# Reordering the beginning of a fused spectral-filter and MLP kernel: one load queue, shared evacuations, transpose mode, and the places of the weight conversions

## The chip, the cores and the metric

One core of one Trainium2 chip. The metric is the device time of one execution in microseconds (us); lower is better. The profile is one execution recorded by the hardware profiler; its times are microseconds from the span's start.

## The reference

Eight batches of 3008 rows by 256 columns go through a circular convolution along the rows (a real FFT, a product with a complex filter, the inverse FFT), and every row of the result then through a two-layer MLP with the hard-swish function between:

```python
X = np.fft.rfft(x, axis=1)                       # x: (8, 3008, 256)
Y = X * (filt_r + 1j * filt_i)[None, :, :]       # filters: (1505, 256)
y = np.fft.irfft(Y, n=x.shape[1], axis=1)
h = y.reshape(24064, 256) @ w_in                 # w_in: (256, 2048)
g = h * np.clip(h + 3.0, 0.0, 6.0) / 6.0
out = g @ w_out                                  # w_out: (2048, 256)
```

All data are FP32.

## The kernel before

The FFT of length 3008 = 47 × 64 is done as matrix products with small trigonometric tables: a first transform over the 47 (`wa`), a second over the 64 (`wb`), the product with the filter, and two transforms back (`wi`, then `wai`). Between these the data pass through scratch memory in DRAM (`z_d` between the first two, `g_d` between the last two)[...]. The MLP works on blocks of 512 tokens and, within a block, on eight slices of 256 hidden channels: one slice of one block is a step, and there are 47 × 8 steps. Block 0 is computed plainly (`plain_up`, L537, and `plain_down`, L548); from block 1 on a Strassen form with seven products in place of eight is used (L450 and L526). It needs sums of weight parts, which GpSimd forms (`w_sums`, L252). The work of the following batches' transforms is put into the steps by a plan written out by hand: `at(step, fn, ...)` lists what each step also does, functions in `EARLY` before the second half of the step's matmuls and the others behind them. [...]

The change touches only what comes before block 0 and the plan of block 0 with the first steps of block 1. The beginning has these stages.

- Loads: the start table with an identity matrix and the first-transform table, `x` of batch 0 (`x0_load`, L291, in pieces of 4 or 8 of the 32 column pairs), filter and `wb` tables for six groups (`table_load`, L178 to L181), raw weights (`w_load`, L215), `wi`, `wai` and `wa`. Sync, ScalarE and GpSimd all issue loads. Groups 2 to 5 of the tables go into memory where `x` of batch 0 lay, so they wait until it has been read.
- First transform of batch 0 (`a0_unit`, L300): eight units of 8 matmuls; each unit fills two PSUM banks out of four, and ScalarE copies them out (L302).
- For each of six groups: `turn` (L312: eight 128×128 matmuls with the identity as the moving operand, which transpose the data; ScalarE copies out, L314), `b_unit` (L355), `f_unit` (product with the filter on VectorE, L367 to L369), `bi_unit` (L387; copied out at L390) and `g_store` (L396, to DRAM).
- `t4_load` (L418) brings the stored data back in another layout, `n_unit` (L425; copied out at L431) does the last transform for the first chunks of tokens. `keep_warm` (L643) issues matmuls on zeros while TensorE has nothing else.
- Weights: 16 parts have to be converted before they are used (`w_conv`, L226 to L245: the bits of a pair of words are put together to one FP32 number; seven or eight VectorE operations of 128×512 for each part, and with `act` one on ScalarE). Part 2p is `w_in` of slice p, part 2p + 1 `w_out`. A part's raw bits wait in buffers of other tiles (`W_AT`), and a buffer takes the next part only when the one before it has been converted: that wait stands on the queue that issues the load.

Before the change three parts are converted beside the first transform, two beside the last transform, and eleven in block 0, two in each step from the first on (`at(i // 2, convert, 1)`). In block 0, a step's hswish (L500, VectorE, two for each step) reads the PSUM bank that the next step's `plain_up` writes, so the next step cannot begin before the hswish has run, and the hswish stands on VectorE behind the conversions of the step before last.

Of the kernel before, what the change touches and what calls it, by code (L numbers as in the profile page):

```python
# [23 lines left out]
NA = 47  # L24
NC = 64
KH = 24
# [81 lines left out]
def kernel(  # L108
# [60 lines left out]
    def table_load(b, c, qs=(nc.sync, nc.sync)):  # L169
        if b == 0 and c >= FB:  # L170

            at = x0_at(1536 * (c - FB), 1536)
            t, wb = at[:, 0:1024].rearrange("p (k d) -> p k d", k=TC), at[:, 1024:].rearrange("p (k m) -> p k m", k=TC)
        else:
            t, wb = ft[(b * NT + c) % FB], tabp.tile([P, TC, P], FP32, name="wb")
        st["ft", b, c] = t
        for q, src, p0 in ((qs[0], filt_r, 0), (qs[1], filt_i, HALF)):
            q.dma_start(t[p0:p0 + 32, :, :].rearrange("p k d -> p (k d)"),  # L178
                              raw(src, c * TC, [[NA * D, 32], [1, TC * D]]))
            q.dma_start(t[p0 + 32:p0 + 64, :, :], raw(src, NA - c * TC, [[NA * D, 32], [-D, TC], [1, D]]))  # L180
        qs[c % 2].dma_start(wb, wb_d[:, ts(c, TC), :])  # L181
        st["wb", b, c] = wb
# [103 lines left out]
    def x0_load(j, n):  # L286
        rows = x[0].rearrange("(a c) d -> a c d", c=NC)
        nc.vector.memset(x0[32:64, j:j + n, :], 0.0)
        for a, m in (0, 32), (32, NA - 32):
            for h, q in ((0, nc.sync), (1, nc.gpsimd)):  # L290
                q.dma_start(x0[h * 64 + a:h * 64 + a + m, j:j + n, :], rows[a:a + m, ds(h * HC + j, n), :])  # L291

    def zt(dh):
        return (xn.rearrange("p a n -> p (a n)"), xs.rearrange("p i j d -> p (i j d)"))[dh]

    def a0_unit(j):
        for dh in range(2):
            ps = bank(0)
            for u in range(4):
                nc.tensor.matmul(ps[:, ts(u, P)], x0[0:64 + NA, j + u, ts(dh, P)], st["start"][0:64 + NA, ts(1, P)],  # L300
                                 start=True, stop=True)
            nc.scalar.activation(out=zt(dh).rearrange("p (n j) -> p j n", j=HC)[:, j:j + 4, :],  # L302
                                 in_=ps.rearrange("p (j n) -> p j n", j=4)[:, :, 0:4 * KH], func=AXT.Copy)

    def turn(c):
        t = t2p.tile([P, TC, D], FP32, name="t2")
        for v in range(2):
            ps = psU.tile([P, 512], FP32, name=("al", "be")[v])
            for u in range(2):
                for dh in range(2):  # L310
                    k = c * TC + 2 * v + u
                    nc.tensor.matmul(ps[:, ds(u * D + dh * P, P)], zt(dh)[:, ts(k, P)], st["start"][:, 0:P],  # L312
                                     start=True, stop=True)
            nc.scalar.activation(out=t[:, 2 * v:2 * v + 2, :].rearrange("p k d -> p (k d)"), in_=ps, func=AXT.Copy)  # L314
# [65 lines left out]
    def bi_unit(b, i):  # L380
        ys = [st.pop(("y", b, i + v)) for v in range(2)]
        ps = [psF.tile([P, 2, D], FP32, name="psf", tag="f") for ri in range(2)]
        for v in range(2):
            for ri in range(2):

                w, y = (wi[ts(ri, 64), 0, :], ys[v][ts(ri, 64)]) if b else (wi[:, 1 + ri, :], ys[v][ri])
                nc.tensor.matmul(ps[ri][ts(v, 64)], w, y, start=True, stop=True)  # L387
# [5 lines left out]
    def g_store(b, i, qs=(nc.gpsimd, nc.gpsimd)):  # L393
        t = st.pop(("t3", b, i))
        for v in range(2):
            qs[v].dma_start(g_d[b, i + v].rearrange("ri u c d -> c (ri u) d"), t[ts(v, 64)].rearrange("p ri u d -> p (ri u) d"))  # L396
# [219 lines left out]
    with tc.manual_schedule():  # L616
# [4 lines left out]
        two = (nc.sync, nc.gpsimd)  # L621
# [5 lines left out]
        nc.vector.memset(half_c, 0.5)  # L627
        loaded = done = 0

        def convert(n, act=True, most=NCONV, q=nc.sync):  # L630
            nonlocal loaded, done
            for i in range(n + 1):
                while loaded < most and w_before(loaded) < done:
                    w_load(loaded, q)
                    loaded += 1
                if i < n:
                    w_conv(done, act)
                    done += 1
# [6 lines left out]
        convert(0, most=2, q=nc.scalar)  # L645
        nc.scalar.dma_start(wi, wi_d)
        nc.scalar.activation(out=zero[:, 0:1], in_=half_c, func=AXT.Copy)
        keep_warm(5)
        for j, n in (0, 4), (4, 4), (8, 8), (16, 8), (24, 8):
            x0_load(j, n)  # L650
        convert(0, most=3, q=nc.gpsimd)
        nc.gpsimd.memset(t4, 0.0)
        for c in range(FB):
            table_load(0, c, two)
        for j in range(0, HC, 4):
            a0_unit(j)
        convert(3, False, 5)
        for c in range(FB, NT):
            table_load(0, c, two)
        convert(0, most=8)  # L660
        nc.sync.dma_start(wai[:, 0:8, :], wai_d[:, 0:8, :])
        for i in range(3):
            w_sums(i, False)
        turn(0)
        for c in range(NT + 1):
# [6 lines left out]
            if c:  # L672
                bi_unit(0, 2 * c - 2)
                g_store(0, 2 * c - 2, (nc.scalar, nc.scalar) if c < NT else (nc.scalar, nc.sync))
# [3 lines left out]
        keep_warm(16)  # L678
        convert(2, False)
# [3 lines left out]
        for c in range(3):  # L683
            x_load(1, c)
        nc.sync.dma_start(wai[:, 8:HC, :], wai_d[:, 8:HC, :])
        nc.sync.dma_start(wa, wa_d)
        for i in 3, 4:
            w_sums(i, False)


        for i in range(NCONV - done):
            at(i // 2, convert, 1)
            at(i // 2 + 1, w_sums, done + i, False)
        for p in range(NP):
            for i in range(2):
                at(p + 2, w_sums, 2 * p + i, True)

# [17 lines left out]
        def places(n):  # L715
# [6 lines left out]
            if n == 1:  # L722
                a_at = list(range(1, NB + 1))
# [126 lines left out]
```

## Time and profile before

| | |
|---|---|
| median of 3 runs | 2766.2 us (2765.32 to 2770.9) |
| span of the profiled execution | 2764.2 us |
| TensorE matmuls busy | 2716.7 us (98%) |
| VectorE busy | 1951.5 us (71%) |
| ScalarE busy | 1332.9 us (48%) |
| GpSimd busy | 408.4 us (15%) |
| DMA | 194.74 MB, mean 70 GB/s |
| first matmul of `plain_up` / first matmul of block 1 | 89.06 / 166.16 us |

Busy shares are means over the whole span. The change concerns the first 170 us or so, so the views that count are those of that stretch: the chain of waits in order of time (start, length, engine and line of each piece), the timeline (start, length, engine, line, operation, and in brackets the idle time before it and what ended it), and the windows (for each stretch the busy time of each engine with its instructions, the granted TensorE clock, the share of the DMA engines and the GB/s). Each FP32 matmul shows as two rows of TensorE.

### The profile page before, as it was taken

The numbers are of one execution on the slowest core, as the hardware profiler recorded it, in microseconds if no ns is written. First come the engines' busy times: TensorE is split into PE (matmuls) and PEld (weight loads), VectorE is DVE, ScalarE is ACT, GpSimd is POOL, SyncE is SP. The second block draws the span as 40 slices with busy tenths as digits, with TensorE's granted clock in tenths as the row PEclk, the third lists the DMA queues.
The fourth block names the chain that finished last, engine by engine and source line by source line (L and its number), as shares of the span: only waits on it lengthen the run. The fifth ranks groups of instructions, "written<-read, shape, count | busy, mean of one in ns | idle before, by whom it ended". The sixth has DMA issues, their size and how long they took to land.

```text
span 2764.2 us, 47162 instructions
## 1 busy us (share of the span) xinstructions
PE 2716.7 (98%) x18154; PEld 2412.4 (87%) x18154; DVE 1951.5 (71%) x3404; ACT 1332.9 (48%) x2665; POOL 408.4 (15%) x640
## 2 busy tenths in 40 slices
PE   8999999999999999999999999999999999999997
PEld 6478888999889988899889998899988999999997
DVE  7657766777567775678756787567775777766665
ACT  4234455444554455544554445544455444545443
POOL 2341112010211002110121001210012100100000
PEclk9999999999999999999999999999999999999999
DMA  8633223221332213322133212332123321100000
GB/s 220 169 100 89 60 70 88 62 76 50 85 91 70 60 41 89 89 73 54 46 92 90 69 50 56 91 100 69 35 60 91 92 72 38 42 24 24 18 9 16
DMA packets 117827, 194.74 MB, mean 70 GB/s; under 512 B 21805, under 2 KB 82349, under 8 KB 117193
## 3 DMA queue, kind: packets, MB, share of 16 engines
q1 hardware_dynamic: 94397, 138.68, 17.7%
q0 software_dynamic: 19088, 48.65, 7.7%
q10 hardware_dynamic: 4118, 4.39, 0.6%
q8 instruction: 144, 2.36, 0.4%
q14 instruction: 80, 0.66, 0.1%
HBM read 119.80 MB, written 71.83 MB: 69 GB/s over the span
## 4 chain that ended last, share of the span: by engine, by line
PE 93%; DVE 3%; DMA 2%; issue 0%; ACT 0%; SPq 0%; POOL 0%; ACTq 0%; POOLq 0%; DVEq 0%
PE po L526 42%; PE al L450 23%; PE be L450 17%; PE psn L425 4%; PE psf L355 3%; PE psf L332 2%; PE psf L387 2%; DMA w_all<-wb_t 1%; DVE g L500 0%; DMA w_all<-in_x_dram 0%; PE po L548 0%; PE po L300 0%; PE al L537 0%; DMA t<-g_tmp 0%; DVE y L229 0%
## 5 line engine op out<-in xcount | busy, mean ns | idle before, releaser
L526 PEld LDWEIGHTS po<-w_all,g 128*128 128x128 f32 x10304 | 1369.5, 192 | 142.6 <-issue 38.3
L526 PE MATMUL po<-w_all,g 128*128 128x128 f32 x10304 | 1399.6, 276 | 4.4 <-DVE g L500 4.4
L500 DVE SCALAR_TENSOR_TENSOR g<-r,h 128x512 f32<-128x512 f32 x736 | 506.7, 688 | 269.5 <-ACT r L495 257.0
L495 ACT ACTIVATE r<-h,half_c 128x512 f32<-128x512 f32 x736 | 531.2, 722 | 329.7 <-DVE h L476 317.7
L450 PE MATMUL al<-xt,w_all 128*128 128x256 f32 x2208 | 660.5, 381 | 2.1 <-DVE h L481 1.6
L476 DVE TENSOR_TENSOR h<-be,s 128x512 f32<-128x512 f32 x368 | 254.2, 691 | 264.8 <-PE be L450 253.5
L450 PE MATMUL be<-xn,w_all 128*128 128x256 f32 x1472 | 437.8, 379 | 0.0
L450 PEld LDWEIGHTS al<-xt,w_all 128*128 128x128 f32 x2208 | 335.5, 192 | 4.1 <-DVE h L481 2.3
L450 PEld LDWEIGHTS be<-xn,w_all 128*128 128x128 f32 x1472 | 279.7, 190 | 37.9
L490 ACT ACTIVATE h<-al 128x256 f32<-128x256 f32 x368 | 141.3, 384 | 350.3 <-PE al L450 350.3
L481 DVE TENSOR_TENSOR h<-al,s 128x256 f32<-128x256 f32 x368 | 156.3, 425 | 166.1 <-PE al L450 164.9
L508 DVE TENSOR_TENSOR g<-g 128x512 f32<-128x512 f32 x368 | 255.1, 693 | 12.7
L471 ACT ACTIVATE s<-al 128x256 f32<-128x256 f32 x368 | 141.4, 384 | 200.3 <-PE al L450 200.3
L462 ACT ACTIVATE s<-be 128x256 f32<-128x256 f32 x368 | 141.4, 384 | 176.3 <-PE be L450 176.3
L450 PE MATMUL al<-xn,w_all 128*128 128x256 f32 x736 | 219.9, 381 | 0.5 <-ACT h L490 0.5
L450 PE MATMUL be<-xt,w_all 128*128 128x256 f32 x736 | 218.9, 379 | 0.0
L344 POOL DMA_DIRECT2D z_tmp<-t x224 | 130.2, 585 | 421.4 <-ACT t L335 393.6
L461 ACT ACTIVATE s<-al 128x256 f32<-128x256 f32 x368 | 141.4, 384 | 70.9 <-PE al L450 70.9
L510 DVE TENSOR_TENSOR g<-g 128x256 f32<-128x256 f32 x368 | 160.6, 436 | 12.5
L507 DVE TENSOR_TENSOR g<-g 128x256 f32<-128x256 f32 x368 | 156.8, 426 | 12.6
L450 PEld LDWEIGHTS be<-xt,w_all 128*128 128x128 f32 x736 | 139.8, 190 | 18.9
L582 POOL TENSOR_TENSOR o<-p,o 128x256 f32<-128x256 f32 x45 | 32.7, 728 | 813.1 <-ACT t L390 381.1
(121 smaller groups left out, 1908.8 us busy)
## 6 DMA issues: line engine op xcount, KB each, us to landing
t<-g_tmp SPq DMA_DIRECT2D x188, 120.0 KB
z_tmp<-t POOLq DMA_DIRECT2D x224, 96.0 KB, 3.1
t<-z_tmp SPq DMA_DIRECT2D x42, 512.0 KB
g_tmp<-t POOLq DMA_DIRECT2D x84, 256.0 KB, 3.8
out_dram<-o SPq DMA_DIRECT2D x321, 47.0 KB
xs<-in_x_dram SPq DMA_DIRECT2D x112, 128.0 KB
ft<-in_filt_r_dram SPq DMA_DIRECT2D x88, 128.0 KB
wb<-wb_t SPq DMA_DIRECT2D x43, 256.0 KB
```

The costliest lines, as they stand in the source:

```text
L450: nc.tensor.matmul(ps, w_in[p][:, w, :], x, start=start, stop=stop, skip_group_check=True)
L461: nc.scalar.activation(out=s[:, 0, :], in_=al, func=AXT.Copy)
L462: nc.scalar.activation(out=s5, in_=be[:, 1, :], func=AXT.Copy)
L471: nc.scalar.activation(out=s[:, 1, :], in_=al, func=AXT.Copy)
L476: nc.vector.tensor_tensor(out=st["h"][0].rearrange("p (a n) -> p a n", a=2), in0=be, in1=s, op=ALU.add)
L481: nc.vector.tensor_tensor(out=st["h"][1][:, 256:512], in0=al, in1=s5, op=ALU.add)
L495: nc.scalar.activation(out=r, in_=st["h"][i], func=AXT.Relu, bias=half_c, scale=1.0 / 6.0)
L500: nc.vector.scalar_tensor_tensor(out=st["g", k, p][:, o:o + 2, :].rearrange("p a n -> p (a n)"), in0=st["r", i], scalar=1.0, in1=st["h"][i ...
L507: v.tensor_tensor(out=g[:, G1, :], in0=g[:, G3, :], in1=g[:, G22, :], op=ALU.add)
L508: v.tensor_tensor(out=g[:, G3:G2 + 1:2, :], in0=g[:, G3:G1 + 1, :], in1=g[:, G11:G11 + 1, :].broadcast_to([P, 2, 256]), op=ALU.subtract)
L510: v.tensor_tensor(out=g[:, G4, :], in0=g[:, G12, :], in1=g[:, G2, :], op=ALU.subtract)
L526: nc.tensor.matmul(st["po", k][bank][:, part, u, :], g[:, a, ts(u, P)], w_out[p][:, w, :], start=(p == 0 and n in OPENS and u == 0), stop= ...
```

## The change

It has five parts. Line numbers of the changed kernel are some 3 to 17 higher.

- All loads up to block 0 go out from Sync, in the order in which they are used; before, they were split between Sync, GpSimd and ScalarE. `x` is loaded in eight equal pieces, with weight part 0 behind the second and part 1 behind the fourth. Two zero fills for padding rows move from VectorE to GpSimd.
- VectorE copies out some of the PSUM banks: those with `dh` = 1 of the first transform, except in units 8 and 12, and one bank of the first `turn`.
- `turn` uses TensorE's transpose mode (`nc.tensor.transpose`) in place of a matmul with the identity.
- Two conversions are beside the first transform and three beside the last, and eleven in block 0 again, at other steps: 0, 0, 1, 2, 2, 3, 4, 4, 5, 5, 6.
- Smaller moves: the matmuls of `bi_unit` fill one bank first and then the other; both halves of each `g_store` of batch 0 go out from ScalarE; the loads of `x` of batch 1 and of the rest of `wai` are put into the plan; the first transform of batch 1 begins at step 2 in place of 1; `keep_warm` has 2 and 9 matmuls in place of 5 and 16.

The diff, cut to its core:

```diff
-        nc.vector.memset(x0[32:64, j:j + n, :], 0.0)
         for a, m in (0, 32), (32, NA - 32):
-            for h, q in ((0, nc.sync), (1, nc.gpsimd)):
-                q.dma_start(x0[...], rows[...])
+            for h in range(2):
+                nc.sync.dma_start(x0[...], rows[...])
...
-            nc.scalar.activation(out=zt(dh)..., in_=ps..., func=AXT.Copy)
+            copy(dh and j not in (8, 12), zt(dh)..., ps...)
...
-                    nc.tensor.matmul(ps[...], zt(dh)[:, ts(k, P)], st["start"][:, 0:P],
-                                     start=True, stop=True)
-            nc.scalar.activation(out=t[...], in_=ps, func=AXT.Copy)
+                    nc.tensor.transpose(ps[...], zt(dh)[:, ts(k, P)], st["start"][:, 0:P])
+            copy(c == 0 and v == 1, t[...], ps)
...
-        for v in range(2):
-            for ri in range(2):
+        for v, ri in ((0, 0), (1, 0), (0, 1), (1, 1)):
...
-        convert(0, most=2, q=nc.scalar)
-        nc.scalar.dma_start(wi, wi_d)
         nc.scalar.activation(out=zero[:, 0:1], in_=half_c, func=AXT.Copy)
-        keep_warm(5)
-        for j, n in (0, 4), (4, 4), (8, 8), (16, 8), (24, 8):
-            x0_load(j, n)
-        convert(0, most=3, q=nc.gpsimd)
-        nc.gpsimd.memset(t4, 0.0)
+        nc.scalar.dma_start(wi, wi_d)
+        keep_warm(2)
+        for j in range(0, HC, 4):
+            x0_load(j, 4)
+            load_bits({4: 1, 12: 2}.get(j, 0))
         for c in range(FB):
-            table_load(0, c, two)
+            table_load(0, c)
+        load_bits(3)
         for j in range(0, HC, 4):
             a0_unit(j)
-        convert(3, False, 5)
+            convert(j in (4, 12), False)
+        nc.gpsimd.memset(t4, 0.0)
         for c in range(FB, NT):
-            table_load(0, c, two)
-        convert(0, most=8)
+            table_load(0, c)
+            if c == 3:
+                load_bits(4)
+        load_bits(5)
         nc.sync.dma_start(wai[:, 0:8, :], wai_d[:, 0:8, :])
+        load_bits(8)
+        nc.sync.dma_start(wa, wa_d)
...
-                g_store(0, 2 * c - 2, (nc.scalar, nc.scalar) if c < NT else (nc.scalar, nc.sync))
+                g_store(0, 2 * c - 2, nc.scalar)
...
-        keep_warm(16)
-        convert(2, False)
+        keep_warm(9)
+        convert(3, False)
...
-        for c in range(3):
-            x_load(1, c)
-        nc.sync.dma_start(wai[:, 8:HC, :], wai_d[:, 8:HC, :])
-        nc.sync.dma_start(wa, wa_d)
-        for i in 3, 4:
+        for i in range(2, done):
             w_sums(i, False)
-        for i in range(NCONV - done):
-            at(i // 2, convert, 1)
-            at(i // 2 + 1, w_sums, done + i, False)
+        at(0, x_load, 1, 0)
+        for i, s in enumerate((0, 0, 1, 2, 2, 3, 4, 4, 5, 5, 6)):
+            at(s, convert, 1)
+            at(s + 1, w_sums, done + i, False)
...
+        at(0, wai_load)
+        for c in 1, 2:
+            at(c, x_load, 1, c)
...
-                a_at = list(range(1, NB + 1))
+                a_at = list(range(2, NB + 2))
```

## The prediction

> **What bounds the kernel now.** I read the page first, for the chain of waits of the whole span, and then only the beginning, since the edits end with token block 0: the chain in order of time, the timeline, and windows of 10 us.
>
> The page says that TensorE carries the span:
>
> ```profile
> PE 93%; DVE 3%; DMA 2%; issue 0%; ACT 0%; SPq 0%; POOL 0%; ACTq 0%; POOLq 0%; DVEq 0%
> ```
>
> The first matmul of block 1 starts at 166.16 us. The remaining 2,598 us are TensorE back to back in both kernels, so what the beginning loses or gains goes one to one into the end. The chain shows where those 166 us go (start, length, what):
>
> ```profile
> 5.84 10.99 DMA w_all<-in_x_dram
> 16.97 10.67 PE po L300 x79
> 27.64 16.29 DMA w_all<-wb_t
> 44.07 1.97 PE po L355 x8
> 46.04 0.89 PE al L312 x8
> 46.93 0.89 PE be L312 x8
> 47.82 1.87 PE psf L387 x8
> 49.70 1.92 PE po L355 x8
> ...
> 66.46 4.72 DMA g_tmp<-t
> 71.25 0.61 SPq L418
> ...
> 73.85 3.46 DMA g_tmp<-t
> 77.38 4.19 DMA t<-g_tmp
> 81.58 3.40 DMA xs<-in_x_dram
> 85.00 2.89 PE psn L425 x20
> ```
>
> Four stages are to be seen. (1) Until 16.97 the first transform waits for x; its last matmul ends at 29.56 in the timeline. (2) From 29.6 to 67.8 turn (L312), second transform (L355) and filter product back (L387) follow each other at a period of 49.70 − 44.07 = 5.6 us, all TensorE, after a table that came 2.67 us late at 44.07. (3) From 67.8 to 85.0 there is only a store, a store and a load; warm-up matmuls fill part of it. (4) Then block 0, where VectorE sets the pace. The timeline shows it by the first hswish of successive steps:
>
> ```profile
> 105.16 0.68 DVE L500 SCALAR_TENSOR_TENSOR g<-r,al 128x512 f32<-128x512 f32 x1
> ...
> 105.90 2.42 PE L537 MATMUL al<-xn,w_all 128*128 128x512 f32 x4 [2.77 <-DVE g L500]
> ...
> 115.37 0.68 DVE L500 SCALAR_TENSOR_TENSOR g<-r,al 128x512 f32<-128x512 f32 x1
> ...
> 125.84 0.68 DVE L500 SCALAR_TENSOR_TENSOR g<-r,al 128x512 f32<-128x512 f32 x1
> ```
>
> A step with two conversions takes 10.2 to 10.5 us (9.1 for the two, 1.2 for two hswish); TensorE's own part is 1.72 + 1.72 (L537) + 3.7 (L548) + 1.0 (L332) = 8.1 us, so it waits about 2.3 us a step.
>
> The windows say what stands behind stages 1 and 2 (the last two columns are the DMA share and GB/s):
>
> ```profile
> 20.00:30.00 10.00, 9.95 (x79) 9.66 (x78) 5.00 (x10) 8.31 (x11) 3.51 (x7) 0.90 1.04 236
> 30.00:40.00 10.00, 9.60 (x67) 8.46 (x68) 7.13 (x11) 3.86 (x7) 6.12 (x13) 1.00 1.05 271
> ```
>
> The 16 DMA engines are full at 236 to 271 GB/s: whatever is loaded before it is needed delays what is needed.
>
> [...] the first four warm-up rows come 0.85 us apart from 4.93, the later ones 0.43. [...]
>
> **The change, part by part.**
>
> Order of loads. Before, 1 MB of weights and the tables share the engines with x. After, x comes first (8 pieces of 376 KB, 4 DMAs each), with only two weight parts between. Two limits: the Sync queue issues one DMA each 0.46 us (16.76, 17.23, 17.70 in the timeline), and its third DMA waits for the first zero fill, now 1.76 us instead of 0.91, so until about 3.5 us. Thirty-two more issues at 0.46 give 18.2[...]: last x at 20.5 to 22. By bytes: 3.08 MB x, 1.05 weights, 0.22 small = 4.35 MB at 236 to 271 GB/s from 2 us gives 18 to 20.5. TensorE needs 8 × 1.78 us (16 rows per unit) and starts at about 6, as ScalarE's table load (1.28 us) no longer stands behind four DMA issues (3.38 us before) and two warm-up matmuls take 3.4 us. So it ends one unit and one evacuation after the last x: turning begins at 24, against 29.6. **5.6 saved** (3 to 7).
>
> Evacuations. ScalarE spent 2 × 0.86 = 1.72 us a unit, as much as TensorE's 1.78; now VectorE takes six of the sixteen, beside ScalarE. It hides behind the x loads and I give it nothing of its own. The wait that it adds: the copies of pieces 16 and 20 stand behind a conversion (4.4 us) on VectorE, and TensorE's unit for piece 24 needs their bank. By issue time the second weight part lands near 15, so that copy is free near 20: about when x of 24 arrives. Nothing lost, or 1 us.
>
> Turning. Eight matmuls take 1.78 us; five of the six turns lie in TensorE's period. [...] the weight loads, which the trace has at 0.11 to 0.19 us each, would hold it at 0.9 to 1.5[...]. I take 0.9. TensorE's period becomes 1.92 + 0.9 + 1.87 = 4.7 us; VectorE's is six operations of 0.68 to 0.69 and gaps, 4.3. So 0.9 a period, six periods: **5 saved** (0 to 7), and the late table's 2.7 if tables arrive in time. Do they? By table 5 some 10.1 MB of loads and 1.6 MB of stores have passed: at 250 GB/s, 49 us, and its product is due near 48. Balanced, so I take 2 of the 2.7. The product back then ends near 55.5 instead of 67.8: 12.3 saved in all.
>
> Store and load. The second half of the last store was on Sync and went out at 73.85, behind eight loads that waited for the earlier stores; ScalarE was free at 68.65. Now both halves go from ScalarE: 0.65 us for the second issue instead of 5.2, so 4.5 saved. The loads of x for batch 1 (12) and 1.1 MB of wai followed the last load at once, and the chain ends on xs from 81.58 to 85.00. Now one x piece follows and then a weight load that waits for a conversion: **3 of 3.4 saved**. From the end of the product to L425: 17.2 − 7.5 = 9.7 us, so 65.2; 4.3 us of L425 and its copies: block 0 at 69.5 instead of 89.3. The warm-up, 9 × 0.86 = 7.7 us, ends before that and hides in it.
>
> Block 0. Eleven conversions remain (two now lie in stage 1, three in stage 3, where VectorE idled; before three and two). Their places are 2,1,2,1,2,2,1 in steps 0 to 6 instead of 2,2,2,2,2,1. Three conversions and four hswish in two steps take 3 × 4.55 + 2.4 = 16.1 us, against TensorE's 2 × 8.1: the gaps close. Step by step from 69.5: first hswish done at 76.5, then TensorE and VectorE alternate as the bound, and block 1 begins about 68 us after block 0 instead of 76.9: **9 saved** (4 to 10). GpSimd's sums and z stores (near 60 us of work, 0.97 busy at 140 to 160 before) stay within these 68 us.
>
> One unit of batch 1 (1.05 us of L332) moves from block 0 into block 1: **1 lost**. Its z is read by t2 loads that went out at 185.62, behind 12 us of output stores, so the later step delays nobody.
>
> Sum: 19.8 + 9 − 1 = 27.8; I round down to 27 for small waits: 2766.2 − 27 = 2739.
>
> **The rivals.**
> A. One queue is too slow: issue at 0.46 us and the completion waits[...] set stage 1, tables come late, transposes cost as much as matmuls. For: 66 issues to table 5, engines already full. Against: [...] in order none of it is early. Then stages 1 and 2 save 3, stage 3 7.5, block 0 6: about 2750.
> B. [...] block 0 runs at TensorE's pace: VectorE's 4.3 binds, 2 us more there, 1 in the table wait, 3 in block 0 and the gaps: 2733.
> C. No gain or slower: [...] weight loads that wait for VectorE stand before wai and x for block 0. If L425 of step 3 or the x pieces came a step late each time, three or four waits of 8 us would eat all: 2766 to 2772. For: seven such waits are queued. Against: by my times wai lands near 93, needed near 99.
>
> **How the numbers follow.** My forecast 0.5, A 0.25, B 0.2, C 0.05. The range goes from B's value less 3 (block 0 at its best) to A's plus 2: 2730 to 2752. Faster than 2760.7 needs 5.5 us: all but C, 0.95; same 0.02; slower 0.03.
>
> **What would show it.** The first transform's last row at 22 to 24 us; L317 groups of eight in 0.9 us and not 1.8; a period of 4.7 in stage 2 with no wait for a table; L428 near 65; the first L453 near 138; from there to the end unchanged at 2,598 us. I am wrong if L317 keeps 1.78, if a DMA stands again in the chain between 25 and 55, or if TensorE waits for VectorE over 1 us a step in block 0.

## The result, and the profile after

The changed kernel takes 2751.2 us (median of four executions, 2749.97 to 2751.89) against 2767.71 us (2765.32 to 2770.9) for the kernel before, measured beside it: a ratio of 0.9939, 95% interval 0.9922 to 0.9956. It is faster by 16.5 us. The forecast was 2739, with a range of 2730 to 2752: the direction is right, the time is at the upper end of the range, and the gain is about 60% of the 27 us that were expected.

The page's chain of waits still names TensorE, with one point more than before (PE is TensorE, DVE VectorE, ACT ScalarE, POOL GpSimd, SP Sync; a q marks an engine's issuing of DMAs):

```profile
PE 94%; DVE 2%; DMA 1%; POOL 1%; issue 1%; ACT 0%; SPq 0%; POOLq 0%; DVEq 0%; ACTq 0%
```

So the place to look is again the beginning. The borders of its stages, each the start or end of a row of TensorE in the timeline, in us:

| | before | predicted | after |
|---|---|---|---|
| first transform ends | 29.56 | 24 | 26.14 |
| product back ends | 67.80 | 55.5 | 61.61 |
| last transform (`n_unit`) starts | 85.00 | 65.2 | 77.01 |
| block 0 starts | 89.06 | 69.5 | 82.75 |
| block 1 starts | 166.16 | 137.5 | 153.76 |
| first down product of block 1 | 176.73 | | 167.40 |

At the start of block 1 the gain is 12.4 us of a predicted 28.7, at the first down product 9.3. Here is the chain of waits of the changed kernel in order of time (start, length, what), the same view as was shown of before:

```profile
8.21 5.15 DMA w_all<-in_x_dram
...
13.49 12.66 PE po L305 x96
...
36.22 1.97 PE po L359 x8
...
40.92 1.93 PE po L359 x8
...
44.55 4.00 DMA w_all<-wb_t
48.69 3.29 PE po L359 x8
...
70.53 3.62 DMA t<-g_tmp
74.63 2.40 DMA xs<-in_x_dram
77.03 4.55 PE psn L428 x20
```

Two groups of the second transform (L359) follow each other at 40.92 − 36.22 = 4.7 us, as predicted, in place of 5.6. But DMAs still stand in the chain, at 8.21, at 44.55 and, two in a row, from 70.53 on, and two rows are longer than their work: L359 takes 3.29 us instead of 1.97, and L428 4.55, where it took 2.89 before. The timeline says what ended TensorE's idle time before each of them (start, length, engine, line, operation, in brackets the idle time and its end):

```profile
13.49 12.65 PE L305 MATMUL po<-p,w_all 111*128 111x128 f32 x96 [2.50 <-DMA w_all<-in_x_dram]
...
48.69 3.29 PE L359 MATMUL po<-t,w_all 128*128 128x256 f32 x8 [3.10 <-DMA w_all<-wb_t]
...
77.01 4.98 PE L428 MATMUL psn<-wai,t 128*128 128x94 f32 x22 [7.48 <-DMA xs<-in_x_dram]
...
99.27 2.73 PE L540 MATMUL al<-xn,w_all 128*128 128x512 f32 x4 [3.98 <-DVE g L503]
...
159.80 0.67 PE L453 MATMUL al<-xt,w_all 128*128 128x256 f32 x2 [2.50 <-ACT s L474]
```

Five waits, 19.6 us together. The name at 77.01 is not the cause: L428 reads no x, and the two loads of x land only at 76.96 and 77.14. The last load of `t`, issued at 71.92, lands at 76.56; TensorE's wait for it ends at 76.59, and some more waits that were already met take it to 77.01. The view puts a wait for several DMAs down to one of them.

The clock comes on top: beside the first three waits it is at half for 3.41 us (15.03 to 18.45), 3.41 us (49.16 to 52.58) and 13.65 us (73.06 to 86.71), and once more for 3.41 us from 100.36. The windows of 10 us show the last (stretch, length, then the busy time of PE, PEld, DVE, ACT and POOL, the granted clock, the DMA share and GB/s):

```profile
70.00:80.00 10.00, 2.99 (x14) 3.02 (x15) 4.33 (x8) 0.53 (x1) 3.00 (x6) 0.65 0.30 89
80.00:90.00 10.00, 9.77 (x25) 5.31 (x25) 1.58 (x3) 3.28 (x8) 0.00 (x0) 0.66 0.06 20
```

In the second window TensorE is busy for 9.77 of 10 us and yet works at a clock of 0.66: busy time alone doesn't show this loss.

### The profile page after: what moved, and what is told of

Its sections match the earlier page's. It is cut to its first block, busy times and chain, and to the rows that moved or that the text cites. A ratio compares the mean times of both kernels' runs of the same rounds, so it can differ in the third digit from the quotient of the medians.

```text
span 2750.0 us, 47026 instructions
## 1 busy us (share of the span) xinstructions
PE 2703.0 (98%) x18086; PEld 2404.5 (87%) x18086; DVE 1948.8 (71%) x3407; ACT 1327.2 (48%) x2658; POOL 398.8 (15%) x616
## 3 DMA queue, kind: packets, MB, share of 16 engines
q1 hardware_dynamic: 97383, 143.89, 18.2%
## 4 chain that ended last, share of the span: by engine, by line
PE 94%; DVE 2%; DMA 1%; POOL 1%; issue 1%; ACT 0%; SPq 0%; POOLq 0%; DVEq 0%; ACTq 0%
PE po L529 42%; PE al L453 23%; PE be L453 17%; PE psn L428 4%; PE psf L359 3%; PE psf L336 2%; PE psf L390 2%; POOL w_all L252 0%; PE po L305 0%; PE po L359 0%; DMA xs<-in_x_dram 0%; DMA t<-g_tmp 0%; DVE g L503 0%; PE po L551 0%; POOL z_tmp L348 0%
```

## The experiments

Six questions came out of this: whether the half clock before block 0 costs what it seems to, why the table at 48.69 is late, what the transposes are worth, what holds the stores and loads between 62 and 77 us, whether the places of the conversions shorten block 0, and what the wait at 159.80 comes from. The borders of all runs (the letters stand for the rows of the table above; runs that start from the kernel before are marked *b*):

| run | F: first transform ends | E: product back ends | N: L428 starts | U: block 0 | K: block 1 | D: first down product | time | ratio to before, 95% |
|---|---|---|---|---|---|---|---|---|
| after | 26.14 | 61.61 | 77.01 | 82.75 | 153.76 | 167.40 | 2751.2 | 0.9922 to 0.9956 |
| e1_warm17 | 25.20 | 60.97 | 75.59 | 78.91 | 147.87 | 163.20 | 2748.72 | 0.9920 to 0.9950 |
| e2_pool_stores | 25.08 | 57.87 | 72.62 | 78.36 | 148.18 | 161.79 | 2747.63 | 0.9917 to 0.9946 |
| e3_matmul_turn | 27.34 | 63.17 | 80.20 | 85.93 | 156.65 | 173.30 | 2754.91 | 0.9938 to 0.9971 |
| e4_old_steps | 24.80 | 61.55 | 75.54 | 81.27 | 158.75 | 170.43 | 2754.76 | 0.9940 to 0.9970 |
| e5_late_bits | 24.91 | 61.84 | 74.30 | 80.03 | 150.58 | 164.25 | 2748.57 | 0.9918 to 0.9948 |
| e6_before_turn *b* | 28.05 | 66.09 | 83.91 | 88.75 | 166.37 | 176.94 | 2763.05 | 0.9979 to 0.9992 |
| e7_units_early | 25.10 | 61.44 | 75.57 | 81.31 | 167.78 | 180.40 | 2766.57 | 0.9994 to 1.0012 |
| e8_before_last_store *b* | 27.59 | 68.07 | 81.84 | 85.15 | 159.69 | 170.26 | 2759.2 | 0.9969 to 0.9986 |
| e9_sums_later | 27.03 | 63.07 | 77.98 | 83.71 | 154.25 | 166.72 | 2750.26 | 0.9924 to 0.9954 |
| e10_pool_matmul | 24.89 | 60.06 | 74.50 | 80.24 | 151.81 | 167.12 | 2751.52 | 0.9934 to 0.9961 |
| c1_all | 25.81 | 56.97 | 69.87 | 73.26 | 142.12 | 154.56 | 2744.33 | 0.9912 to 0.9939 |
| c2_x_first | 24.51 | 56.46 | 70.23 | 73.62 | 143.43 | 155.77 | 2742.66 | 0.9906 to 0.9933 |

The first transform is the same code in ten of the runs and ends between 24.80 and 27.34 us, so the borders themselves can shift by 2.5 us without a reason in the edit. The lengths of the stages between them are what is to be compared, and they vary too: E to N is 13.99 to 17.03 us in six runs whose loads and stores there are the same (after, e1, e3, e4, e7, e9). The runs were measured in four groups after the changed kernel; the kernel before took 2765.9 to 2767.2 us beside them and 2767.7 beside the changed kernel, so that a difference between medians of two groups can be off by up to 1.8 us. But for e7, the intervals of single edits of the changed kernel overlap with its own: their verdicts rest on the one trace of each.

**The clock before block 0.**

```diff
-        keep_warm(9)
+        keep_warm(17)
```

> The changed kernel with 17 warm-up rows instead of 9 before the inner products of block 0. My theory ([...] 7.48 us idle before L428 and then 13.65 us at half clock, of which some 4.9 us are lost): the rows end near 76.5 us, just before the last load lands, L428's first 22 rows take 3.3 us instead of 4.98, the first plain_up 1.9 instead of 3.7, and block 1 starts 4 to 5 us earlier than 153.76, near 149; time about 2747 us. Rival 1 (VectorE's conversions pace steps 0 and 1, TensorE waits 3.98 us for it in step 1 anyway): the clock is full but block 1 starts at 152.5 or later and the time stays at 2750 to 2751. Rival 2 (the half clock comes from the gaps of block 0, not from the idle time): a half-clock stretch of 13 us stays.

The timeline of this run:

```profile
60.90 14.86 PE L652 MATMUL al<-r 128*128 128x512 f32 x34
75.59 2.59 PE L428 MATMUL psn<-wai,t 128*128 128x94 f32 x22
...
78.91 1.91 PE L540 MATMUL al<-xn,w_all 128*128 128x512 f32 x4
```

There is no idle time in front of L428, and no half clock until 93.77. From N to U it takes 3.32 us instead of 5.74, and from U to K 68.96 instead of 71.01: 4.5 us, as the theory had it, and block 1 starts at 147.87. Both rivals fall. From K to D 1.7 us are lost again to a new half-clock stretch at 155.21, so that N to D is 2.8 us shorter; the median is 2.5 us lower.

**The late table.** The waits of the Sync queue in the changed kernel up to 60 us (in total, times, longest):

```profile
SPq L215 <- DMA g_tmp<-t: 4.6, 1, 4.6
...
SPq L178 <- DMA g_tmp<-t: 2.0, 1, 2.0
```

A load of raw weights (L215) and a load of a filter table (L178) waited for a store of `g_tmp` to land. Neither reads `g_tmp` nor writes where the store reads. In the trace each goes out as one of ScalarE's stores lands: the weights at 40.14, when the store of 36.81 had landed at 40.12, and the table at 46.92, when that of 41.62 had landed at 46.86. Once Sync stood in line behind ScalarE's stores, the tables behind it were late as well. What ties a load to a store that it doesn't touch these views do not show; the next run tests whether the wait goes when ScalarE no longer issues the stores.

```diff
-                g_store(0, 2 * c - 2, nc.scalar)
+                g_store(0, 2 * c - 2, nc.gpsimd if c < NT else nc.scalar)
```

> The changed kernel with the stores of filter products of batch 0 issued by GpSimd instead of ScalarE, but for the last group. My theory ([...] Sync stood 4.6 and 2.0 us behind stores that had not landed, and the table of group 4 came 3.1 us late): Sync has no such wait between 30 and 50 us, TensorE no wait for a table over 0.5 us, no half clock at 49, and the product back ends 3 to 4.5 us earlier, at 57 to 58.6 instead of 61.6; the end gains the same, about 2747.5 us. Rival (the DMA engines are full, at a share of 1.0, and the table is as late whoever issues the stores): TensorE still waits 2 to 4 us at 48.7 and the time is 2750 to 2752. A third way: the product back ends earlier, but L428 waits for the same loads (72 to 77 us), and nothing is gained at the end.

Sync's two waits are gone (what it waits for g_tmp now is at L421, which reads it). The timeline at the place where the table had been late:

```profile
44.73 1.94 PE L390 MATMUL psf<-s,wi 128*64 128x512 f32 x8
46.59 1.99 PE L359 MATMUL po<-t,w_all 128*128 128x256 f32 x8
48.42 0.27 PE L317 MATMUL al<-p,xn 128*128 128x128 f32 x1
```

L359 follows L390 without a gap and at full clock. The product back ends at 57.87, 3.7 us earlier (1.1 of it in the first transform, which the edit doesn't touch); L428 4.4 us earlier; block 1 5.6 us earlier; the median falls by 3.6. So the loads were late by their order and by Sync's waits for ScalarE's stores, not by the bytes: the engines carried 305 GB/s between 36 and 50 us in this run, against 237 in the changed kernel. The "engines full" rival falls. Part of the expectation missed: an earlier group still waits 1.02 us for its table, at 37.29.

**The transpose mode.** In the kernel after, the eight transposes of a turn take 0.89 us and stand 0.11 us apart; before, the eight matmuls took 1.78. Undone in the changed kernel, in the kernel of e2, and done alone in the kernel before:

```diff
-                    nc.tensor.transpose(ps[...], zt(dh)[:, ts(k, P)], st["start"][:, 0:P])
+                    nc.tensor.matmul(ps[...], zt(dh)[:, ts(k, P)], st["start"][:, 0:P],
+                                     start=True, stop=True)
```

> The changed kernel with its turns as matmuls with the identity again. Theory of the prediction (0.89 us a turn at full worth, six turns): the product back ends 5 us later, at 66.6, and the time is 2756. Theory after the trace (the late table of group 4 hides most: TensorE reaches it 3.6 us later and its wait of 3.10 us and the half clock after it go): the period is 5.6 instead of 4.7, the table's wait under 0.5 us, the product back ends at 62.5 to 64, and block 1 starts 1 to 2.5 us later than 153.76; time 2752 to 2753.5. Rival (it is hidden altogether behind the loads of stage 3): L428 at 77 and time 2751.

> The changed kernel with the stores of batch 0 issued by GpSimd (e2) and the turns as matmuls with the identity (e3). Theory (the transposes are worth 0.9 us a turn, and e3 hid it only behind the late table): from the first matmul of the second transform to the end of the product back 34 to 34.5 us, against 29.4 in e2, and the time 4 to 5 us over e2's 2747.6: about 2752. Rival (VectorE or the loads set the period in e2 anyway): 31 us or less, time 2748 to 2749.5.

> The kernel before with nothing changed but the turns, in transpose mode. Theory (0.9 us for each turn that lies in TensorE's chain; the two turns ahead of the table that came 2.67 us late gain nothing, since the table is as late): the product back ends 3 to 4 us earlier, at 64 to 65 instead of 67.8, and block 1 starts as much earlier than 166.16; time about 2764, ratio 0.9987. Rival 1 (all six count, as the prediction took it): 5 us, 2762. Rival 2 (the stores and loads of stage 3 swallow it): L425 stays at 84.5 to 85 and the time at 2767.

From the first L359 to the end of the product back the changed kernel takes 33.35 us (28.26 to 61.61) and e3 33.27 (29.90 to 63.17): in that stage, which has five of the six turns, the transposes gain nothing. The wait of 3.10 us for group 4's table is not there in e3; only a later one of 0.64 us is. With the table in time it is otherwise: 29.42 us in e2 (28.45 to 57.87) and 32.60 in e10 (27.46 to 60.06), which is 3.2 us; between the medians it is 3.9 us (2751.52 and 2747.63). That is less than the 4.6 to 5 expected, for e2 waits 1.02 us for a table at 37.29 and e10 doesn't. (A wait of 1.50 us in e2, at 28.45, lies ahead of the stage; counted from the end of the first transform, 2.4 us are left of the 3.2.) Alone in the kernel before, the transposes take the stage from 35.64 us to 34.49, 1.1 us, since the wait for the table grows from 2.67 to 3.98 us and the clock halves behind it:

```profile
43.42 3.25 PE L354 MATMUL po<-t,w_all 128*128 128x256 f32 x8 [3.98 <-DMA w_all<-wb_t]
```

The time fell by 3.6 us there (0.9979 to 0.9992), near what was expected, but from L425 on that one trace shows no more than 1.1 us and at block 1 none, so where the median's gain comes from isn't shown. The same holds for e3: it is 3.7 us slower than the changed kernel, and its trace, the slowest of its four executions (2758.26), has the loss outside of the stage with the turns (1.2 us in the first transform and 0.4 up to the first L359, 1.6 between E and N, 3.0 between K and D, where the clock was at half for 6.83 us from 161.95).

**The stores and loads before block 0.** In the kernel before, the second half of the last store went out late from Sync. Moved to ScalarE alone:

```diff
-                g_store(0, 2 * c - 2, (nc.scalar, nc.scalar) if c < NT else (nc.scalar, nc.sync))
+                g_store(0, 2 * c - 2, (nc.scalar, nc.scalar))
```

> The kernel before with nothing changed but the last store of block 0's filter product: both halves from ScalarE instead of one from ScalarE and one from Sync. Theory of the prediction (the half on Sync went out at 73.85, behind eight loads; 4.5 us): L425 starts 12.7 us after the product back instead of 17.2, block 1 4.5 us earlier, time 2762. Rival (what ends the stage is the small loads after it, which go out and land one by one, and the twelve x loads behind them): L425 1 to 2.5 us earlier, 14.7 to 16.2 us after the product back, time 2764.5 to 2766.

The timeline of this run:

```profile
68.00 14.00 PE L643 MATMUL al<-r 128*128 128x512 f32 x32
81.84 2.59 PE L425 MATMUL psn<-wai,t 128*128 128x94 f32 x22
```

N comes 13.77 us after E instead of 17.20: 3.4 us, between the two expectations. The trace has more: the last load lands at 80.40 and all waits of L425 are met at 80.69; what holds it then are the last of the 16 warm-up matmuls. From the product back to the landing of the last load it is 12.3 us instead of 16.9, which is the 4.5 of the prediction. And since the warm-up of this kernel now reaches to L425, the clock is full too; block 1 starts 6.5 us earlier and the median falls by 6.7 us. In the kernel before, this one line is worth 40% of what the whole change gained; in the changed kernel it was not undone. In the changed kernel the same stage takes 15.40 us. What stood in its way is seen on ScalarE:

```profile
55.77 1.25 ACTq L399 DMA_DIRECT2D g_tmp<-t  x2
...
62.76 1.08 ACT L393 ACTIVATE t<-psf 128x512 f32<-128x512 f32 x2 [3.22 <-DMA g_tmp<-t]
63.87 1.36 ACTq L399 DMA_DIRECT2D g_tmp<-t  x2
70.53 2.03 ACTq L421 DMA_DIRECT2D t<-g_tmp  x2
```

A store issued at 55.77 holds the buffer `t3` for some 7 us, and the copy into it waits until 62.76; the window shows why it took so long (same columns as above):

```profile
50.00:60.00 10.00, 10.00 (x42) 5.40 (x41) 7.79 (x12) 3.47 (x6) 0.00 (x0) 0.87 1.01 344
```

The DMA engines are full. Four weight parts of 512 KB (4 to 7), which block 0 needs only later, are 2.1 of the 3.4 MB in this stretch. Parts 5 to 7, and `wa`, moved behind the loads of block 0:

```diff
-        load_bits(8)
-        nc.sync.dma_start(wa, wa_d)
         for i in range(2):
             w_sums(i, False)
...
+        load_bits(8)
+        nc.sync.dma_start(wa, wa_d)
         keep_warm(9)
```

> The changed kernel with weight parts 5 to 7 and wa (1.6 MB) loaded after the loads of block 0's transform values instead of before the turns. My theory (between 50 and 62 us the DMA engines are full at 334 GB/s with loads that nobody needs yet, so the stores of groups 3 and 4 take 7 us, ScalarE waits 3.22 us for one, and the last stores go out late): the store of group 4 lands 4 us sooner, ScalarE's wait at 62.76 is under 0.5 us, L428 starts 15.4 - 3 = about 12 us after the product back instead of 15.4, the end gains 2 to 3.5 us: 2748 to 2749. Rival (stage 3 is set by the small loads and their landing one by one, not by bytes): L428 still 15 us after the product back, 2751. Second rival (the parts now reach VectorE late): TensorE waits over 3.98 us in step 1 or again in step 2, and what stage 3 gains is given back: 2751 or slower.

The copy before the last store, in the timeline of this run:

```profile
61.16 1.31 ACT L393 ACTIVATE t<-psf 128x512 f32<-128x512 f32 x2 [1.40 <-PE psf L390]
62.50 1.25 ACTq L399 DMA_DIRECT2D g_tmp<-t  x2
```

It waits for TensorE alone. E to N is 12.46 us, 2.9 less than in the changed kernel and 1.5 less than in e4, the shortest of the runs with the same loads and stores; the median falls by 2.6. TensorE's wait for VectorE, 3.98 us at 99.27 in the changed kernel, stays at 3.97 us (it is there in all runs of the changed kernel but e7, where it is 2.76, and no edit was aimed at it). The theory holds and both rivals fall. The wait for the late table is still there (4.32 us), which again says that it is not these bytes.

**The conversions in block 0.**

```diff
-        for i, s in enumerate((0, 0, 1, 2, 2, 3, 4, 4, 5, 5, 6)):
+        for i, s in enumerate((0, 0, 1, 1, 2, 2, 3, 3, 4, 4, 5)):
```

> The changed kernel with its eleven conversions in block 0 placed two a step (2, 2, 2, 2, 2, 1) as before, instead of 2, 1, 2, 1, 2, 2, 1. Theory of the prediction (VectorE paces a step with two conversions at 10.2 us against TensorE's 8.1, so the spreading is what shortens block 0): TensorE waits about 2 us for VectorE in steps 2 to 5, block 0 lasts 76 to 77 us instead of 71.0, block 1 starts 4 to 6 us later, near 159, and the time is about 2756. Rival (GpSimd's sums and z stores set the end of block 0, as its chain there is POOL and z_tmp): block 1 starts at 153 to 155 and the time is 2751 to 2752.

Block 0 (U to K) takes 77.48 us instead of 71.01. The first rows of its steps in the timeline:

```profile
107.32 1.98 PE L540 MATMUL al<-xn,w_all 128*128 128x512 f32 x4
...
117.80 1.98 PE L540 MATMUL al<-xn,w_all 128*128 128x512 f32 x4
...
128.12 1.98 PE L540 MATMUL al<-xn,w_all 128*128 128x512 f32 x4 [0.15 <-DVE g L503]
...
139.38 3.78 PE L540 MATMUL al<-xn,w_all 128*128 128x512 f32 x4 [2.88 <-DVE g L503]
```

and the next at 150.64; in the changed kernel they stand at 109.17, 119.55, 129.45, 137.56 and 145.66. The first two distances are nearly the same in both, 10.5 and 10.3 against 10.4 and 9.9: each of these steps also has a last transform (L428, 1.25 us) and a slower L336 (1.67 to 2.03 us, 1.09 in the others), so that TensorE fills it by itself. All of the loss is in the next two, 11.3 and 11.2 us instead of 8.1: 3.0 us of waiting for VectorE, and the half clock that follows it (138.74 to 145.57; L540 takes 3.78 instead of 1.98). So the spreading does carry block 0, but through two steps and the clock, not through 2 us in each. At the border 2 us come back (K to D is 11.68 instead of 13.64, and TensorE's wait there 0.55 instead of 2.50), so that from U to D 4.5 us remain; the median is 3.6 us higher. The rival falls for block 0 and is right for the border.

**The border to block 1.** The change moved the first transform of batch 1 by one step, and the prediction booked this as 1 us lost. The trace shows ScalarE waiting there for a store that GpSimd issues behind its weight sums:

```profile
153.63 1.09 ACT L339 ACTIVATE t<-psf 128x512 f32<-128x512 f32 x2 [3.65 <-DMA z_tmp<-t]
...
158.30 1.08 ACT L339 ACTIVATE t<-psf 128x512 f32<-128x512 f32 x2 [2.65 <-DMA z_tmp<-t]
```

Two edits, one for each cause:

```diff
-                a_at = list(range(2, NB + 2))
+                a_at = list(range(1, NB + 1))
```

> The changed kernel with the first transform of batch 1 one step earlier again (steps 1 to 8 instead of 2 to 9). Theory of the prediction (each unit costs TensorE 1.05 us wherever it stands, so moving one between the blocks moves 1 us from one to the other): block 0 1 us longer, from the first matmul of block 1 to its first down product 1 us shorter, the time the same, 2751. My theory after the trace (the z stores of these units stand behind the weight sums on GpSimd and cost 2.5 us at 159.80; one step earlier they are out before block 1): TensorE's wait at the border is under 0.5 us, first L453 to first L529 10.5 to 11.5 us instead of 13.6, the end 1.5 to 2.5 us earlier: about 2749. Rival (earlier units meet late x pieces and wai in block 0): TensorE waits for DMA xs in steps 1 to 4 and the time is 2752 or more.

```diff
-                at(p + 2, w_sums, 2 * p + i, True)
+                at(p + 5, w_sums, 2 * p + i, True)
```

> The changed kernel with the late weight sums of part p at step p + 5 instead of p + 2 (each is needed at step p + 8). My theory (GpSimd's queue at the end of block 0 is full of weight sums, and the z stores behind them hold ScalarE's copies 1.85, 3.65 and 2.65 us): ScalarE's waits for z_tmp at 140 to 160 are under 1 us each, TensorE's wait of 2.50 us at 159.80 is under 0.5, first L453 to first L529 about 11 us instead of 13.6, the end 2 to 2.6 us earlier: 2748.5 to 2749. Rival (the sums now come too late for block 1): TensorE waits for POOL w_all in steps 8 to 12 and the time is 2751 or more.

The first was a surprise, and the largest effect of the study. One step earlier costs 15.4 us (2766.57 us), the whole gain of the change. The timeline of TensorE:

```profile
113.02 2.38 PE L336 MATMUL psf<-xs,wa 47*64 47x512 f32 x8 [10.48 <-DMA xs<-in_x_dram]
```

and the issues of Sync, in the same view:

```profile
105.31 0.44 SPq L215 DMA_DIRECT2D bits<-in_moe_w_out_dram  x1
105.80 4.34 SPq L275 DMA_DIRECT2D xs<-in_x_dram  x7
```

The second piece of x for batch 1 goes out at 105.80, because on Sync it stands behind eight loads of `t` and behind weight loads, each of which waits until VectorE has converted the part that holds its buffer (24.5 us of such waits between 75 and 130 us, 29.1 in the changed kernel). The wait of 10.48 us also takes the clock to half until 118.05; another wait for x, 1.50 us, follows at 126.39, and the clock is at half again from 128.3 on. With the unit itself, these make up the 15.5 us by which block 0 is longer, to within 2 us. In the changed kernel that piece goes out at 105.58, just as late, but it isn't needed until the step after. The rival of the expectation is what came true, far larger than it had it. The second edit brings ScalarE's wait of 2.65 us down to 1.48 and TensorE's from 2.50 to 1.33; K to D is 12.47 us instead of 13.64, half of what was expected, and the median (2750.26) can't be told from 2751.2.

**Together.** Stores from GpSimd, weight parts behind the loads, fourteen warm-up matmuls, later sums:

> The changed kernel with four edits together: stores of batch 0 from GpSimd, weight parts 5 to 7 and wa behind the loads of block 0, fourteen warm-up rows, and the late weight sums three steps later. Theory (the waits are in series, so the gains add: 4 us for the clock, 4 to 5.5 for the table, 3 for the stores, 1 for the sums): product back at 58, L428 at 70 to 71 and at full clock, block 1 at 142 to 143, time 2739 to 2741. Rival (each wait that goes uncovers the next: an x piece or a weight part that comes late behind Sync's waits, as the 10.48 us for DMA xs in the run with the earlier units): block 1 at 146 or later, time 2744 or more.

```profile
56.90 12.28 PE L652 MATMUL al<-r 128*128 128x512 f32 x28
69.87 2.66 PE L428 MATMUL psn<-wai,t 128*128 128x94 f32 x22 [0.68 <-DMA t<-g_tmp]
...
87.80 2.56 PE L540 MATMUL al<-xn,w_all 128*128 128x512 f32 x4 [3.97 <-DVE g L503]
```

Block 1 starts at 142.12 and the first down product is 12.8 us earlier than in the changed kernel: in this one trace the waits are in series, and their gains add. The five executions lie between 2740.80 and 2748.54 us, all below those of the changed kernel; the profiled one is the 2740.80, so the median of 2744.33, a gain of 6.9, is the fairer figure: the times show 6.9 of the 10 to 12 us that were expected. The median lies at the rival's value, though the trace shows nothing of the rival's late pieces; what the slower executions lost is open.

**The wait for x at 13.49**, last, with weight parts 0 and 1 behind later pieces of x:

```diff
-            load_bits({4: 1, 12: 2}.get(j, 0))
+            load_bits({16: 1, 24: 2}.get(j, 0))
...
-            convert(j in (4, 12), False)
+            convert(j in (16, 24), False)
```

(and on c1's edits; ScalarE copies 20 and 28 in place of 8 and 12, and both banks of the first turn).

> The run with four edits together (c1), and weight parts 0 and 1 loaded behind x pieces 16 and 24 instead of 4 and 12; their conversions stand behind the copies of 16 and 24, ScalarE takes the copies of 20 and 28 and both copies of the first turn. Theory (the 1.8 us by which the prediction missed stage 1, and more, is the 2.5 us that TensorE waited at 13.49 for the x piece behind weight part 0, and the half clock after it): no wait of TensorE for x over 1 us before the turns, the last row of the first transform at 22.5 to 23.5 us, block 1 2 to 3 us earlier than 142.12, time 2741 to 2742 if c1 stands at 2744. Rival (the rate at which x arrives, not its order, sets stage 1): the wait moves to later pieces, and the last row stays at 25 to 26. Second rival: the later conversions hold VectorE's products of the second transform and stage 2 gives back what stage 1 gains, time 2744 or more.

```profile
17.81 3.81 PE L305 MATMUL po<-p,w_all 111*128 111x128 f32 x32 [1.45 <-DMA w_all<-in_x_dram]
22.49 2.02 PE L305 MATMUL po<-p,w_all 111*128 111x128 f32 x16 [0.87 <-DMA w_all<-in_x_dram]
```

The wait of 2.5 us becomes two, of 2.3 us together: it moves, as the rival said. What goes is the half clock, as each wait is short. The stage ends at 24.51 instead of 25.81, within the spread of that border, and block 1 is no earlier. So this run doesn't show that the order of these loads cost the missing 2 us; the rate at which x arrives may have. At 2742.66 us (2741.89 to 2746.03) this is the best version run, not separable from c1, and faster than both kernels of the study: its longest execution (2746.03) lies below the shortest of the changed kernel (2749.97).

That VectorE shares the copies was not tried alone. In the trace TensorE runs 96 rows of L305 from 13.49 on without a wait, so nothing is lost by it; what it brings is open. The same holds for the one load queue in place of three, the zero fills on GpSimd and the new order of `bi_unit`. Nor do all loads of the changed kernel go out from Sync: ScalarE issues the start table, `wi` and two of the last loads of `t` (70.53 and 71.92), the second of which is the one that L428 waits for.

## Why the prediction came out too low

The parts of the change that were tried do what they were said to do, and the work that TensorE sets by itself came out as worked out: 0.89 us a turn, a period of 4.7, a step of 8.1. What failed is in the waits between, and with them the sizes and their order (predicted 5.6, 6.7, 7.5 and 9 for the four stages, measured 3.4, 2.8, 1.8 and 6.1). A sign that the prediction named against itself came true: a DMA in the chain between 25 and 55, at 44.55. Another, waits for VectorE over 1 us a step in block 0, did in one step (3.98 at 99.27). That the time lies in the range is in part luck, as the last point shows. Point by point, in us:

- **First transform, 5.6 saved.** Measured 3.4 (2.2 to 4.8 over the other runs with the same first stage). The term took the last piece of x as the only limit and left out what an earlier wait costs: 2.50 at 13.49, and 1.7 of half clock behind it. That the order of the loads is its cause is not shown (c2). The time between the last issue (18.2) and the last x (20.5 to 22) was the author's estimate; in the changed kernel the last load of x took 3.43, from 20.55 to 23.98. The waits for the zero fill and for VectorE's copies were as expected.
- **Turning, 5 saved and 2 of the late table's 2.7.** The price was right: 0.89 against 0.9, the period 4.7. The step that failed is "balanced, so I take 2": the table was 3.10 late with 1.7 of half clock, and hid the transposes. Stage 2 gained 2.8 instead of 6.7. The count of bytes was the wrong measure. Waits for a landing, which rival A counted on in stage 1, held Sync 4.6 and 2.0 behind ScalarE's stores here, and e2 shows that without this the stage from the first L359 on is 3.9 shorter, and that the transposes are then worth 3.2 there.
- **Last store, 4.5, and the x loads, 3 of 3.4.** Measured together 1.8. The first was right: in e8 the last load lands 4.5 sooner, and 3.4 of it reach L425. In the changed kernel part was given back, for it fills the engines with weight parts at the time of the last stores: 1.5 to 2.9 by e5. The second misread the chain. Its piece of 3.40 at 81.58 names x, but L425 reads no x: in that trace too the wait is for the last load of `t`, issued at 78.84 and landed at 84.69, and ends at 84.73. Without the weight loads E to N is still 12.46, not 9.7, because the last small loads go out from 68.45 on, six us after the issue of the last store, and the last of them, issued at 69.94, takes until 74.10. The prediction had no term for that landing.
- **"The warm-up ends before that and hides in it."** This is the step of which the words are true and the conclusion false. The nine warm-up matmuls end at 69.5, 7.5 before L428, and TensorE pays 4.5 for that in L428 and block 0 (e1). The change itself cut them from 16 to 9; the prediction asked only whether they stand in the way. The kernel before paid as well: its clock was at half for 6.83 from 86.84 on.
- **Block 0, 9 saved, 68 long.** Measured 6.1 saved, 71.0 long; 68.96 in e1 and 68.86 in c1, where the clock is full as block 0 begins. The step was right, and most of its shortfall is the clock's. e4 shows that it is the places of the conversions that carry it, though in two steps where TensorE waits and its clock halves, not by 2.3 in each step as the prediction read it. The timeline of the kernel before has this already: of its waits for the hswish only those at 105.90 (2.77) and 148.15 are long; those at 126.57 (0.30) and 136.90 stand behind steps with a last transform.

```profile
136.90 1.98 PE L537 MATMUL al<-xn,w_all 128*128 128x512 f32 x4 [0.16 <-DVE g L500]
148.15 3.68 PE L537 MATMUL al<-xn,w_all 128*128 128x512 f32 x4 [2.88 <-DVE g L500]
```

- **The unit moved to block 1, 1 lost.** K to D grew by 3.07: 1.05 for the unit, as taken, and 2.0 more of waiting (2.50 at 159.80, 0.55 before). But the step looked at one side: without this move the x pieces, which the change put behind weight loads, would have held TensorE for 10.48 (e7). It is a necessary part of the change.
- **The rest unchanged, 2,598.** 2596.2 in the profiled execution, but only because two differences cancel: 3.07 lost from K to D, and 4.8 gained from D to the end (2587.4 before, 2582.6 after), which nobody forecast. The kernel before has a half-clock stretch at 240.4, two waits of 0.69 for a copy of ScalarE (257.50 and 306.62) and one of 0.94 for a load (2090.34) which the changed kernel hasn't, and 1.6 lie behind the last matmul. From D to the end the eleven traces with the change take 2582.5 to 2584.5, the kernel before, e6 and e8 2585.6 to 2587.4. Which part of the change brings this, if one does, is open. Without these 4.8 the time would have been near 2756 (an estimate: 2751.2 and 4.8), outside the range.

Rival A, 2750, met the number, and its completion waits are in the trace (4.6 and 2.0 for stores); but its sum was another one (3 + 7.5 + 6 against 6.2, 1.8 and 6.1, less 1.7 between N and U). Rival C's mechanism, weight loads on Sync that wait for VectorE ahead of x, is there too (29.1 us of such waits in the changed kernel, 24.5 in e7), one step away from costing everything.

How long TensorE may be idle before its clock halves doesn't follow from these traces. Idle times of 0.68 and 1.56 before L428 (c1, c2) left it full. In the changed kernel it was at half for 3.41 us each after 2.50 (at 13.49) and 3.10 (at 48.69), but stayed full after 2.50 at 159.80; after 7.48 it came back only 9.7 us after L428 had begun, as the last section shows.

## What to carry to other kernels

When an edit shortens what comes before a wait, ask of everything that filled the wait (warm-up matmuls, loads for later) whether it still fits: here a shorter warm-up and loads put in early cost 4.5 and some 2 to 3 us of a predicted 28. Where a wait is for several DMAs, look up which one landed last before you believe the name beside it. Don't put a load that waits for an engine ahead of one that TensorE needs on the same queue (TensorE waited 10.48 us in e7), and look up what a queue's loads wait for before they go out, not only how many bytes there are: here Sync stood 4.6 and 2.0 us behind ScalarE's stores. And test a move that seems to cost a little by undoing it: the one booked as 1 us lost was worth 15.

## What the runs showed of the hardware

- All half-clock stretches here are multiples of 3.41 us, but for the one at the end of each trace. Those around the last transform grow with the idle time before it: 0.68 us none (c1), 1.56 none (c2), 4.54 and 6.83 us 10.24 (e5, e2), 6.99 and 7.48 us 13.65 (e9, after), 9.10 us 17.07 (e3). But what grows is mostly the part that falls into the idle time itself. In all ten runs with such a stretch it begins 2.1 to 5.1 us after TensorE falls idle and ends 7.8 to 10.1 us after the transform has begun, with TensorE busy nearly throughout: 8.7 us after an idle time of 3.27 (before), 9.7 after 7.48 (after), 10.1 after 9.10 (e3). Behind the wait of 10.48 us in e7, where matmuls of 512 columns follow, it ends after 5.0 us. So the length of the idle time does little to the way back; whether the matmuls of 94 columns are what makes it long is not shown.
- A transpose in transpose mode on FP32 tiles of 128×128 comes each 0.11 us, twice as fast as the matmul with the identity (0.22).
- Loads of only 24 KB, to four partitions, took 2.7 to 4.6 us from issue to landing (issued from 68.37 to 71.92 in the changed kernel).
